# Batch 1's state softmax from token-partition scores, sums of exponentials on GpSimd, and a new order of every step

## The chip, the cores and the metric

The kernel runs on one core of one Trainium2 chip. The core has five instruction streams that run side by side and wait for each other by semaphores: TensorE (PE, with its weight loads shown apart as PEld), VectorE (DVE), ScalarE (ACT), GpSimd (POOL) and SyncE (SP, which here only issues transfers). The metric is the device time of one execution in microseconds; each time given is a median of runs.

## The reference, cut to what matters

A block with two stages. The first is a cross attention between tokens `x` (8 batches, 8 heads, 512 tokens, 64 wide) and a small state (32 rows per head): tokens read the state, and the state rows read the tokens. Both results are laid behind each other, 544 rows of 512 per batch. The second stage is a two-layer network with a leaky activation over all 4352 rows.

```python
scores = scale * x @ state.T            # per batch and head, 512 x 32
a = softmax(scores)                     # over the 32 state rows
xread = a @ state
a2 = softmax(scale * state @ x.T)       # over the 512 tokens
sread = a2 @ x
X = concat([xread, sread], rows)        # heads side by side: 544 x 512 per batch
h = X @ w_in                            # 512 -> 2048
g = max(h, 0) + alpha * min(h, 0)
out = g @ w_out                         # 2048 -> 512
```

## The kernel before, in words

All is unrolled by hand. `ORDER` is a string of some 1250 tokens; a loop at the end calls one small function per token, and manual scheduling keeps that order on every engine. So each engine runs its own instructions strictly in the order in which the tokens stand, and an instruction whose input is late holds up all that stand behind it on its engine. The last numbers of a token choose one of the eight PSUM banks or a slot of a buffer.

The work by token, with its line in the kernel before:

- Loads, issued by GpSimd (they cast to f16): `lx` one batch of `x` (L201), `wi` and `wo` a quarter of each weight (L253, L259), `lst` the states (L247). `xd` (L327) is a transfer issued by SP that writes `x` transposed into `xT`; for batches 0 and 1 TensorE transposes instead (`xt`, L340). `tt` (L541) transposes the exponentials `e2` by a transfer.
- Scores: `sc` (L362) puts the scores of one batch with states in partitions into two banks. They feed the softmax over tokens: `tm` maximum on DVE (L514), `te` exponentials on ACT (L527), then `rd` (L553) reads the tokens.
- The softmax over the 32 state rows has two forms. Batches 1 to 7 take the scores of `sc`: `sb` transposes 32x32 blocks on DVE (L466), `smax` maximum on DVE (L476), `ssh` subtracts on GpSimd (L482), `sexp` on ACT (L488). Batch 0 computes its scores a second time on TensorE with tokens in partitions: `sd` (32 small matmuls per half, L409), `hm` maximum on DVE (L420), `hs` subtracts by a matmul with a negative identity (L423), `he` on ACT (L433). Both go on with `ssum`, sum and reciprocal on DVE (L492, L493), `snorm` on GpSimd (L496) and `wb`, a block transpose on DVE (L504).
- `xread` is never formed: `m` (L590) multiplies the states with a 512-wide quarter of `w_in`, `mo` (L603) copies the result to f16 on ACT or DVE, and `F` (L620) multiplies this with the softmax weights: a first-layer tile of 128 hidden units by 512 tokens. `f` is the same in two halves (L641). `N` (L652, ACT) takes the negative part and `G` (L656, DVE) the activation. Batch 8 stands for the state rows of all batches (L629).
- The second layer of batch 0 is plain: `S` (L675), two matmuls of 512 columns each. For the other batches seven products `P` (L793, four matmuls of 256 columns) stand for eight, as in Strassen's scheme. They need sums of hidden blocks, `A` (L765, GpSimd or DVE), and sums of weight blocks, `W` (L745). `C` (L805, ACT or DVE) copies a product out, `D` (L810, DVE) adds one, and `st` (L722, SP) stores 128 rows.
- `Z` (L272) are matmuls of zeros in the first microseconds; nothing reads them.

Buffers that take turns (`xg`, `xT`, `ts`, `e2` and others) come from a pool that hands out its copies in turn.

## Time and profile before

| | |
|---|---|
| median of 3 runs | 208.99 us (208.47 to 209.76) |
| span of the profiled execution, first to last instruction | 205.4 us |
| busy: PE / DVE / ACT / POOL | 197.1 / 181.6 / 145.2 / 159.6 us |
| moved by transfers | 23.22 MB |

The profile shows one execution. The span leaves out what lies around the instructions: the median of the runs is 3.6 us above it, and the steps of the prediction are taken against the span and then carried over by these 3.6 us. An engine's busy time counts matmuls with modelled, overlapping ends, so a PE that is busy all the time can still be slowed; the distance from one matmul to the next is the better measure of its pace. In the windows below, a pair is microseconds busy and the number of instructions.

### The profile page before, as it was taken

The page shows a single profiled execution, that of the slowest core. Times are in us where ns is not written, and L with a number is a line of the kernel's source. Part 1 is how long each engine was busy: PE and PEld are TensorE (multiplying, and loading weights), DVE is VectorE, ACT ScalarE, POOL GpSimd, SP SyncE. Part 2 cuts the span into 40 slices and gives each one's busy share as a digit, 9 for nine tenths or more (in the row PEclk, how much of TensorE's full clock was granted, in tenths as well). Part 3 has the DMA queues.
Part 4 walks back from the last instruction along what each step waited for, and adds up shares of the span by engine and source line. Part 5 has one row for each costly group of instructions (what it writes and reads, how often), then busy time and mean ns, then how long its engine had stood idle before and what let it go on. Part 6 is the DMA issues. An engine that isn't in the chain of part 4 may idle for free.

```text
span 205.4 us, 5181 instructions
## 1 busy us (share of the span) xinstructions
PE 197.1 (96%) x2023; PEld 131.4 (64%) x2023; DVE 181.6 (88%) x321; ACT 145.2 (71%) x319; POOL 159.6 (78%) x136
## 2 busy tenths in 40 slices
PE   7887999999999999999999999999999999999993
PEld 2542344445757766766557776776778777788882
DVE  4799999999999989999899999989999699995841
ACT  2599997889897679899898878869666476411120
POOL 7575489999989979998998899987997988502220
PEclk9999999999999999999999999999999999999999
DMA  5999999995999342749990135022000220031124
GB/s 81 195 203 209 204 206 197 185 232 54 163 163 178 66 153 58 100 103 158 194 163 3 53 123 135 3 105 102 0 0 3 111 93 3 2 131 62 69 102 156
DMA packets 39257, 23.22 MB, mean 113 GB/s; under 512 B 22320, under 2 KB 35008, under 8 KB 39232
## 3 DMA queue, kind: packets, MB, share of 16 engines
q0 software_dynamic: 12704, 8.59, 29.3%
q1 hardware_dynamic: 26496, 14.29, 28.4%
q8 instruction: 16, 0.26, 0.6%
q14 instruction: 9, 0.07, 0.2%
q10 hardware_dynamic: 32, 0.01, 0.0%
HBM read 17.31 MB, written 8.91 MB: 128 GB/s over the span
## 4 chain that ended last, share of the span: by engine, by line
PE 85%; DVE 5%; DMA 5%; POOL 1%; ACT 1%; issue 1%; ACTq 0%; POOLq 0%
PE ps L793 44%; PE ps L620 24%; PE ps L675 7%; DMA xg<-in_x_dram 5%; PE ps L629 3%; PE ps L590 3%; DVE gt_all L656 3%; PE ps L553 1%; ACT neg_all L652 1%; PE ps L362 1%; DVE m_all L603 1%; POOL xg L218 1%; DVE ts L466 1%; DVE nb L514 1%; DVE mx L476 1%
## 5 line engine op out<-in xcount | busy, mean ns | idle before, releaser
L656 DVE SCALAR_TENSOR_TENSOR gt_all<-neg_all,oma_sb,ps 128x512 f16<-128x512 f32 x128 | 89.3, 738 | 3.0 <-ACT neg_all L652 2.7
L652 ACT ACTIVATE neg_all<-ps 128x512 f32<-128x512 f32 (+1 forms) x144 | 77.4, 598 | 20.0 <-PE ps L620 14.4
L620 PE MATMUL ps<-aT,m_all 128*128 128x512 f16 x250 | 66.4, 379 | 0.3 <-DVE m_all L603 0.2
L765 POOL TENSOR_TENSOR hc_all<-gt_all 128x512 f16<-128x512 f16 x43 | 49.2, 1160 | 11.4 <-DVE osb_all L810 8.7
L793 PEld LDWEIGHTS <-hc_all 128*128 128x128 f16 x480 | 46.3, 98 | 14.3 <-issue 1.1
L793 PE MATMUL ps<-wc,hc_all 128*128 128x256 f16 x360 | 47.7, 273 | 0.0
L793 PEld LDWEIGHTS <-gt_all 128*128 128x128 f16 x336 | 32.6, 98 | 8.3 <-issue 0.5
L805 ACT COPY osb_all<-ps 128x256 f32<-128x256 f32 x51 | 19.1, 383 | 25.7 <-PE ps L793 22.2
L620 PEld LDWEIGHTS <-m_all 128*128 128x128 f16 x250 | 24.0, 98 | 18.0 <-issue 2.2
L603 ACT CAST m_all<-ps 128x512 f16<-128x512 f32 x58 | 31.6, 621 | 4.3 <-PE ps L590 4.3
L765 POOL TENSOR_TENSOR hc_all<-gt_all,hc_all 128x512 f16<-128x512 f16 x22 | 25.4, 1164 | 6.3 <-DVE hc_all L765 6.1
L793 PE MATMUL ps<-w_out_sb,gt_all 128*128 128x256 f16 x224 | 29.7, 273 | 0.0
L765 POOL TENSOR_TENSOR hc_all<-hc_all,gt_all 128x512 f16<-128x512 f16 x21 | 24.3, 1164 | 3.9 <-DVE hc_all L765 3.6
L810 DVE TENSOR_TENSOR osb_all<-osb_all,ps 128x256 f32<-128x256 f32 x45 | 18.0, 413 | 7.6 <-PE ps L793 4.7
L496 POOL TENSOR_TENSOR an<-ts,r 128x1024 f16<-128x1024 f32 (+1 forms) x9 | 15.5, 1725 | 6.2 <-DVE r L493 4.0
L482 POOL TENSOR_TENSOR ts<-ts,mx 128x1024 f32<-128x1024 f32 x7 | 13.4, 1918 | 5.4 <-DVE mx L476 5.4
L675 PE MATMUL ps<-w_out_sb,gt_all 128*128 128x512 f16 x64 | 16.6, 380 | 0.1
L793 PE MATMUL ps<-w_out_sb,hc_all 128*128 128x256 f16 x120 | 16.5, 273 | 0.0
L793 PE MATMUL ps<-wc,gt_all 128*128 128x256 f16 x112 | 14.7, 273 | 0.0
L590 PE MATMUL ps<-w_in_sb,stT 64*32 64x512 f16 x256 | 11.8, 383 | 1.9 <-DMA w_in_sb<-in_moe_w_in_dram 0.9
L527 ACT ACTIVATE e<-ps,nb 128x512 f16<-128x512 f32 x16 | 11.1, 705 | 0.1
L675 PEld LDWEIGHTS <-gt_all 128*128 128x128 f16 x64 | 5.9, 98 | 7.2 <-issue 1.2
(78 smaller groups left out, 204.6 us busy)
## 6 DMA issues: line engine op xcount, KB each, us to landing
out_dram<-osb_all SPq DMA_DIRECT2D x33, 256.0 KB, 2.6
xg<-in_x_dram POOLq DMA_DIRECT2D x7, 512.0 KB, 9.1
w_in_sb<-in_moe_w_in_dram POOLq DMA_DIRECT2D x4, 512.0 KB, 12.0
w_out_sb<-in_moe_w_out_dram POOLq DMA_DIRECT2D x4, 512.0 KB, 13.6
xg<-in_x_dram POOLq DMA_DIRECT2D x2, 256.0 KB, 4.5
out_dram<-osb_all SPq DMA_DIRECT2D x2, 128.0 KB, 2.4
gs_all<-in_state_dram POOLq DMA_DIRECT2D x1, 192.0 KB, 6.8
st<-in_state_dram SPq DMA_DIRECT2D x1, 128.0 KB, 2.4
```

The source lines that it names most:

```text
L482: engine(e).tensor_tensor(ts, ts, over_blocks(cols(softmax_tile("mx", b), j, S // N)), ALU.subtract)
L496: engine(e).tensor_tensor(blocks(cols(softmax_tile("an", b), j, S)), blocks(cols(softmax_tile("ts", b), j, S)), over_blocks(cols(softmax_t ...
L590: nc.tensor.matmul(banks[N * k : N * (k + 1), (k0, k1)[g], :], st_head(b, 2 * k + g)[64 * g : 64 * g + 64, :], w_in_sb[64 * g : 64 * g + 6 ...
L603: copier(e)(ms[b, f][:, g, :], banks[:, live["mp", b, f][g], :])
L620: nc.tensor.matmul(h.rearrange("p (r t) -> p r t", r=2), ms[b, f][:, g, 128 * j : 128 * (j + 1)], weights(b, g), start=(g == 0), stop=(g = ...
L652: nc.scalar.activation(neg, h, RELU, bias=0.0, scale=-1.0)
L656: nc.vector.scalar_tensor_tensor(gts[b, f][:, j, :], negs.pop((b, jc)), oma_sb[:, jc : jc + 1], hs.pop((b, jc)), ALU.mult, ALU.add,)
L675: nc.tensor.matmul(outs[b, q], hidden(b, jc, q), w_out_sb[:, jc, :], start=(jc == 0), stop=(jc == n_jc - 1),)
L765: engine(e).tensor_tensor(t, x, y, ALU.add if s == 1 else ALU.subtract)
L793: nc.tensor.matmul(outs[b, i, bank], rows, cols, start=(p in (1, 2, 5) and jc == 0), stop=(jc == n_jc // 2 - 1), skip_group_check=True,)
L805: copier(e)(rows_at(b, q, k)[:, 256 * half : 256 * (half + 1)], outs[b, i, "x"])
L810: nc.vector.tensor_tensor(to, to, outs[b, i, bank], ALU.add)
```

## The change

Batch 1's softmax over the state rows takes the form that batch 0 had (`sd`, `hm`, `hs`, `he`, in two halves) in place of `sb`, `smax`, `ssh`, `sexp`; `sc.1` stays, for the softmax over tokens. The reciprocal becomes a step of its own, `srec`, and `ssum` names its engine: two of the ten sums stay on DVE (the first half of batch 0, and batch 3), eight go to GpSimd as a chain of five additions that halve the width from 32 to 1 (16, 8, 4, 2, 1), with the tile `an` as scratch. `ORDER` is replaced as a whole, so all steps of all engines stand in a new order and many change bank, slot or engine: of 120 `A`, 37 are on DVE instead of 32; of 60 `C`, 18 instead of 9; of 64 `mo`, 9 instead of 6; of 8 `W`, 2 instead of none. The zeros shrink from 21 matmuls to 15. Buffers that took turns now have fixed places in a table, `HOMES`. Functions for joint products, pairs of tiles and double stores (`CC`, `DD`, `su`, `NN`) are added, but no token of `ORDER` calls them.

```diff
-lx0.0 lx0.1 id ni.v wi.0 oma lst stc Z.7.32 stt.2 sto.a lx.1 wi.1 dd.0.0.v wi.2 Z.7.3 xt.0.0.0.6
...
+lx0.1 lx0.0 id lst stc Z.7.20 stt.0 sto.v dd.1.0.a dd.1.1.a dd.0.0.a dd.0.1.a Z.7.11 xt.0.0.1.1 xt.0.1.1.2
...
+HOMES = {
+    "xg": "01232013",
+    "xT": "01010101",
...
+    "e2": "01220120",
+    "e2T": "10001001",
+    "sn": "01000110",
+}
...
+    homes = {
+        kind: [consts.tile(shape, dtype, name=f"{kind}_{i}") for i in range(n)]
+        for kind, (n, shape, dtype) in kinds.items()
+    }
+
+    def home(kind, b):
+        return homes[kind][int(HOMES[kind][b])]
...
-    def state_sum(b, j=None):
+    def state_sum(e, b, j=None):
         r1 = cols(softmax_tile("r1", b), j, S // N)
-        nc.vector.tensor_reduce(r1, blocks(cols(softmax_tile("ts", b), j, S)), AX.X, ALU.add)
+        t = blocks(cols(softmax_tile("ts", b), j, S))
+        if e == "v":
+            nc.vector.tensor_reduce(r1, t, AX.X, ALU.add)
+            return
+        part = cols(softmax_tile("an", b), j, S).bitcast(F32)
+        w = N // 2
+        part = part.rearrange("p (c n) -> p c n", n=w)
+        nc.gpsimd.tensor_tensor(part, t[:, :, :w], t[:, :, w:], ALU.add)
+        while w > 2:
+            w //= 2
+            nc.gpsimd.tensor_tensor(
+                part[:, :, :w], part[:, :, :w], part[:, :, w : 2 * w], ALU.add
+            )
+        nc.gpsimd.tensor_tensor(
+            r1.rearrange("p (c o) -> p c o", o=1), part[:, :, :1], part[:, :, 1:2], ALU.add
+        )
+
+    def state_reciprocal(b, j=None):
+        r1 = cols(softmax_tile("r1", b), j, S // N)
         nc.vector.reciprocal(r1, r1)
```

How the new table moves instructions is shown at three places. The first is GpSimd's queue near the start. Before, from the first weight load on (`w_in_sb` and `w_out_sb` are the weights, `gs_all` first holds the states, `xg_124`, `xg_377` and `xg_443` are batches 1, 2 and 3 of `x`, `an`, `ts` and `r` belong to batch 0's softmax):

```order
L253 DMA w_in_sb<-in_moe_w_in_dram 128x4x512
L247 DMA gs_all<-in_state_dram 128x768
L201 DMA xg_124<-in_x_dram 128x8x256
L253 DMA w_in_sb<-in_moe_w_in_dram 128x4x512 x3
L496 TENSOR_TENSOR an_298<-ts_240,r_0_242 128x512 x2
L259 DMA w_out_sb<-in_moe_w_out_dram 128x4x512 x4
L201 DMA xg_377<-in_x_dram 128x8x256
L201 DMA xg_443<-in_x_dram 128x8x256
```

Now, from the first load of `w_out` on (`xg_69` is batch 2, `xg_70` batch 3, L517 to L523 are one sum of exponentials):

```order
L284 DMA w_out_sb<-in_moe_w_out_dram 128x4x512
L517 TENSOR_TENSOR an_79<-ts_73 128x256
L520 TENSOR_TENSOR an_79<-an_79 128x16x8
L520 TENSOR_TENSOR an_79<-an_79 128x16x4
L520 TENSOR_TENSOR an_79<-an_79 128x16x2
L523 TENSOR_TENSOR r_0_77<-an_79 128x16
L532 TENSOR_TENSOR an_79<-ts_73,r_0_77 128x512 x2
L284 DMA w_out_sb<-in_moe_w_out_dram 128x4x512
L226 DMA xg_69<-in_x_dram 128x8x256
L284 DMA w_out_sb<-in_moe_w_out_dram 128x4x512 x2
L226 DMA xg_70<-in_x_dram 128x8x256
```

Batch 2 of `x` was loaded behind all four quarters of `w_out`; now the last two quarters, and batch 3, stand behind it.

The second place is SP's queue, from its second transfer on. Before (`xT_628` and `xT_793` are the transposed batches 2 and 3, `e2T` the transposed exponentials of batches 0 and 1):

```order
L327 DMA_TRANSPOSE xT_628<-xg_377 128x16x128
L541 DMA_TRANSPOSE e2T_711<-e_0_307 128x8x128
L541 DMA_TRANSPOSE e2T_713<-e_1_416 128x8x128
L327 DMA_TRANSPOSE xT_793<-xg_443 128x16x128
L722 DMA out_dram<-osb_all 128x512 x2
```

Now (`xT_71` is batch 2, `xT_72` batch 3, `e2T_86` and `e2T_87` batches 2 and 0):

```order
L352 DMA_TRANSPOSE xT_71<-xg_69 128x16x128
L352 DMA_TRANSPOSE xT_72<-xg_70 128x16x128
L761 DMA out_dram<-osb_all 128x512
L575 DMA_TRANSPOSE e2T_86<-e_2_85 128x8x128
L575 DMA_TRANSPOSE e2T_87<-e_0_83 128x8x128
```

The two transposed loads come first, and only batch 2's own load releases the first of them.

The third place is TensorE, where it first reads the transposed batch 2. Before, the last steps ahead of it and its first row (`aT_550` are batch 1's softmax weights, `gt_all` the activations):

```order
L620 LDWEIGHTS m_all
L620 MATMUL ps<-aT_550,m_all 128x512
L675 LDWEIGHTS gt_all
L675 MATMUL ps<-w_out_sb,gt_all 128x512
L362 LDWEIGHTS stT
L362 MATMUL ps<-xT_628,stT 32x256
```

Now:

```order
L659 LDWEIGHTS m_all
L659 MATMUL ps<-aT_82,m_all 128x512
L714 LDWEIGHTS gt_all
L714 MATMUL ps<-w_out_sb,gt_all 128x512
L387 LDWEIGHTS stT
L387 MATMUL ps<-xT_71,stT 32x256
```

The neighbours read alike; what moved is how much stands ahead. Before, 26 first-layer steps, 20 second-layer steps and 12 `m` stood ahead of these scores; now 22, 10 and 13 do, with two more `sd` and two more `hs`.

More of the change, by code (lines that the diff above doesn't have):

```diff
@@ L769, in product @@
         bank = {1: "x", 6: "x", 7: "x", 4: "x", 2: "y", 5: "z", 3: "z"}[p]
-        if k is not None:
-            outs[b, i, bank] = single(k, 256)
+        if b in joint:
+            if k is not None:
+                both = outs[b, bank] = single(k).rearrange("p (i c) -> p i c", i=2)
+                for h in range(2):
+                    outs[b, h, bank] = both[:, h]
+            opens = k is not None
+        else:
+            if k is not None:
+                outs[b, i, bank] = single(k, 256)
+            opens = p in (1, 2, 5)
         n = n_jc // 4
@@ L796, in product @@
                 cols,
-                start=(p in (1, 2, 5) and jc == 0),
+                start=(opens and jc == 0),
                 stop=(jc == n_jc // 2 - 1),
@@ L829 @@
     }
-    for token in (globals().get("TOKENS") or ORDER).split():
+    for token in ORDER.split():
         name, *args = token.split(".")
```

299 lines of the change are left out of this document (162 added, 137 removed).

## The prediction

> **What bounds the kernel now.** I read the page for shares, the windows for where each engine is full, and the chain of waits for the pace of TensorE. The page's span, busy times and shares of the chain:
>
> ```profile
> span 205.4 us, 5181 instructions
> PE 197.1 (96%) x2023; PEld 131.4 (64%) x2023; DVE 181.6 (88%) x321; ACT 145.2 (71%) x319; POOL 159.6 (78%) x136
> PE 85%; DVE 5%; DMA 5%; POOL 1%; ACT 1%; issue 1%; ACTq 0%; POOLq 0%
> ```
>
> The windows (us; busy of PE, PEld, DVE, ACT, POOL, each with its instructions; granted clock; DMA share; GB/s):
>
> ```profile
> 10.00:20.00 10.00, 8.17 (x128) 3.70 (x128) 9.46 (x15) 9.13 (x22) 6.80 (x8) 1.00 1.30 204
> 20.00:30.00 10.00, 9.20 (x72) 3.67 (x72) 9.96 (x17) 10.00 (x22) 6.08 (x3) 1.00 1.24 207
> 30.00:40.00 10.00, 10.00 (x48) 4.54 (x47) 10.00 (x15) 7.97 (x16) 9.94 (x5) 1.00 1.28 192
> 40.00:50.00 10.00, 10.00 (x158) 4.44 (x156) 9.83 (x17) 8.72 (x20) 9.63 (x7) 1.00 0.84 155
> ```
>
> Pieces of the chain (start, length, what):
>
> ```profile
> 25.12 1.89 PE ps L675 x8
> 28.15 0.43 PE ps L620 x2
> 180.04 21.85 PE ps L793 x200
> ```
>
> A first-layer step (two L620) takes 0.43 us and the last 200 products take 21.85, 0.109 each for half the columns, so this is one and the same full pace. Up to 25.12, where the second layer starts, TensorE waits on and off for DVE (9.46 and 9.96 of 10) and ACT (9.13 and 10.00); from about 28 to 201.9 it waits for almost nothing. The span is therefore the moment at which TensorE passes a given place in its order, plus the work behind that place. What matters is when it passes, and how much work is added.
>
> **Part by part.** Everything is summed against the span of 205.4; the median of the runs, 208.99, is 3.6 more, which I carry over.
>
> *Added work on TensorE.* Batch 0's token-partition scores show what batch 1's will cost:
>
> ```profile
> L409 PE MATMUL ps<-gs_all,xT 128*32 128x64 f16 x64 | 0.8, 194 | 0.1
> L423 PE MATMUL ps<-gs_all 128*128 128x512 bf16 x2 | 0.8, 376 | 0.1
> ```
>
> 64 small matmuls cost 0.8; the two shifting ones 2 x 0.22 at the pace above (0.8 at the most, as they stand here). That is +1.2 on the bounding engine, between 0 (if they fall into a wait of the start) and +1.6. The six zero matmuls less lie in waits: 0.
>
> *The start.* DVE and ACT gate it, so what they gain there may come back:
>
> ```profile
> L466 DVE STREAM_TRANSPOSE ts<-ps 128x1024 f32<-128x1024 f32 x7 | 8.7, 1243 | 0.0
> L476 DVE TENSOR_REDUCE mx<-ts 128x32 f32<-128x1024 f32 x7 | 8.5, 1209 | 0.0
> L492 DVE TENSOR_REDUCE r<-ts 128x32 f32<-128x1024 f32 x7 | 8.5, 1215 | 0.2 <-ACT ts L488 0.2
> L317 DVE COPY stT<-ps 128x768 f16<-128x768 f16 x1 | 0.9, 905 | 0.0
> L420 DVE TENSOR_REDUCE gs_all<-ps 128x16 bf16<-128x512 f32 x2 | 1.3, 687 | 0.0
> L603 DVE CAST m_all<-ps 128x512 f16<-128x512 f32 x6 | 4.0, 682 | 0.0
> L433 ACT ACTIVATE ts<-ps 128x512 f32<-128x512 f32 x2 | 1.2, 597 | 1.2 <-PE ps L423 1.2
> ```
>
> DVE loses batch 1's transpose 1.24, maximum 1.21 and sum 1.21, half a sum of batch 0 (0.6) and the states' copy 0.91, and gains two maxima (1.37) and two more `m` casts before the first second-layer step (1.36): 5.17 less, 2.73 more, so 2.4 us freed. But ACT, full in the same stretch, takes the states' copy (about as long there, 0.9) and batch 1's two exponentials (1.2) ahead of that step, and gives up the two casts (about 1.3). ACT ends 0.8 fuller. So the return lies between 0 (ACT decides) and 2.4 (DVE decides); ACT is the fuller one by its row, and I take -0.7.
>
> *Sums on GpSimd.* Its priced neighbours:
>
> ```profile
> L496 POOL TENSOR_TENSOR an<-ts,r 128x1024 f16<-128x1024 f32 x7 | 13.4, 1918 | 2.7 <-ACT osb_all L805 1.5 <-ACT neg_all L652 0.7 <-DVE r L493 0.5
> L496 POOL TENSOR_TENSOR an<-ts,r 128x512 f16<-128x512 f32 x2 | 2.1, 1048 | 3.5 <-DVE r L493 3.5
> L765 POOL TENSOR_TENSOR hc_all<-gt_all 128x512 f16<-128x512 f16 x43 | 49.2, 1160 | 11.4 <-DVE osb_all L810 8.7 <-PE ps L574 1.5 <-PE ps L553 0.7
> L745 POOL TENSOR_TENSOR wc<-w_out_sb 128x1024 f16<-128x1024 f16 x4 | 8.5, 2130 | 0.0
> L482 POOL TENSOR_TENSOR ts<-ts,mx 128x1024 f32<-128x1024 f32 x7 | 13.4, 1918 | 5.4 <-DVE mx L476 5.4
> ```
>
> 512 more columns cost 0.87, so a column costs 1.7 ns and an instruction about 0.18 us. A whole batch's chain has 512+256+128+64+32 = 992 columns in five instructions: 1.7 + 0.9 = 2.6 us, against 1.2 on DVE; a half 0.84 + 0.9 = 1.7. Five whole and three half chains add 18. It could be as little as the columns alone (11) or, if narrow pieces cost as a 512-wide instruction does, 8 x 5 x 1.05 = 42; I take 18, by the two rows of the same kind. GpSimd gives up five `A` (5.8), two `W` (4.3) and batch 1's subtraction (1.9): net +6, 166 of some 209 us. Its sums stand a stage ahead of the first-layer steps that need them, whose cover is the products of the batch before. On the path: 0; with cover gone, it is a rival below.
>
> *Switching between small and full matmuls, buffers in fixed places, copies moved from ACT to DVE.* ACT has 29% idle and DVE keeps about its total, 0 each, give or take 0.5 together.
>
> *Batch 2's transposed load.* This decides. For TensorE, SP and GpSimd the rows are (a transfer's row, then its time to landing; the last is TensorE's first read of batch 2):
>
> ```profile
> L259 POOL DMA_DIRECT2D w_out_sb<-in_moe_w_out_dram x2: 762/766/770, 15.0 to 15.7; - x2
> DMA to landing us min/median/max: 14.5/15.4/16.3
> L201 POOL DMA_DIRECT2D xg<-in_x_dram x2: 918/920/922, 16.4 to 17.3; - x2
> DMA to landing us min/median/max: 18.3/19.3/20.3
> L327 SPq DMA_TRANSPOSE xT<-xg x1: 3023/3023/3023, 34.8 to 34.8; - x1
> DMA to landing us min/median/max: 4.6/4.6/4.6
> L327 SPq DMA_TRANSPOSE xT<-xg x1: 1800/1800/1800, 40.7 to 40.7; - x1
> DMA to landing us min/median/max: 4.3/4.3/4.3
> L201 POOL DMA_DIRECT2D xg<-in_x_dram x1: 939/939/939, 55.4 to 55.4; - x1
> DMA to landing us min/median/max: 9.1/9.1/9.1
> L327 SPq DMA_TRANSPOSE xT<-xg x1: 5753/5753/5753, 56.1 to 56.1; - x1
> DMA to landing us min/median/max: 9.6/9.6/9.6
> 41.46 0.41 PE L362 MATMUL ps<-xT,stT 64*32 64x256 f16 x16
> ```
>
> Before, the last two quarters of `w_out` land at 29.5 and 32.0, batch 2 at 34.7 and batch 3 at 37.6, one behind the other; the transposing transfer starts at 34.8, lands at 39.4, and TensorE reads it at 41.5, 2 us later. Now batch 2 is ahead of those two quarters, 2 x 2.5 us earlier: it lands at 29.7. The transposing transfer starts then, with 2.5 + 2.5 + 2.9 = 7.9 us of loads still queued. Alone it took 4.3; beside the last batch of loads 4.6; beside a whole load issued just ahead of it 9.6, and that load 9.1. I take 9.6, since more is queued here than there: landing at 39.3. The bounds are 34.0 (alone) and 41.9 (7.9 of loads first, then 4.3).
>
> The Trainium skill's page "DMA: Bandwidth & Descriptors", section "Issuing engines are not separate DMA queues", says that transfers issued by SP, ACT and GpSimd run on the same 16 DMA engines and interleave; sharing evenly would double 4.6 to an estimated 9.2 and give a time 0.4 shorter than mine. The rows agree.
>
> When does TensorE want it? Ahead of these scores stand four first-layer and ten second-layer steps less than before (14 x 0.43 = 6.0), one `m` (0.4) and the 1.2 more, less the start's 0.7: 41.5 - 6.0 + 0.4 + 1.2 - 0.7 = 36.4. Work behind them: 205.4 - 41.5 + 6.0 - 0.4 = 169.5. So TensorE stands from 36.4 to 39.3, 2.9 us, with 14 steps behind it that need nothing of batch 2. DVE's queue has batch 2's block transpose and then batch 1's remaining activations behind it, so DVE cannot work ahead meanwhile, and the time isn't won back.
>
> Sum: 205.4 + 1.2 - 0.7 + 2.9 = 208.8, that is 39.3 + 169.5; with 3.6 around it **212.4 us**.
>
> A wait of TensorE could cost more than its length. In the windows above the granted clock is 1.00 throughout, and TensorE never stands for 2.9 us there, so no row prices it. The Trainium skill's page "TensorE: Matmul & The Clock Gate", Part 1, says that an idle window of about 3.4 us halves the array's clock until it has been busy about as long. By that page a wait of 2.9 us costs nothing more, and one at the upper bound of the landing an estimated 1.7 us, half a window, on top.
>
> **Rivals.**
>
> *The transposed load is in time (no stall).* Place: the same read. It decides below a landing at 36.4, 6.7 us after the start of the transfer. For it: 4.3 and 4.6 are the commoner times here. Against: neither of these had two whole loads behind it. Then 36.4 + 169.5 = 205.9, or **209.5 us**, no change. Chance 0.25.
>
> *The start pays in full, without a stall.* DVE's 2.4 comes back whole and the added matmuls fall into waits: 205.4 - 2.4 = 203.0, **206.6 us**, faster. For it: DVE is at 9.96 to 10.00 from 20 to 40. Against: ACT at 10.00 in 20 to 30, which gets more. Chance 0.12.
>
> *GpSimd's sums are dear.* At 5.2 us a chain instead of 2.6, batches 2, 4, 5 and 6 add 10.4 between 30 and 150 us, where GpSimd idles 0.1 to 0.4 in 10 by the two windows from 30 to 50, some 3 in all; the `A` that the products wait for then come 7 us late. It decides from about 3.4 a chain, where the idle time is used up. For it: the narrow additions have no row. Against: the two rows above scale with columns. 205.9 + 7.4 = 213.3, **216.9 us**. Chance 0.08.
>
> **The numbers.** The stall of 2.9 us has 0.55; 212.4 is its time. Its bounds run from nothing to 5.5 (215.0), so its own range is 210.5 to 214.5. The range goes down to 206.5, which takes in the case without a stall and the start's full return, and up to 214.5: left out are the dear sums, the latest landings and a start better still, some 0.17. About 1%, 2.1 us, is what a measurement of this kernel can tell from no change: slower is above 211.1, faster below 206.9. Slower: 0.50 of the stall's 0.55 and the 0.08 of the sums, 0.58. Same: 0.25 and the short stalls, 0.30. Faster 0.12.
>
> **What would show it.** A stall: TensorE idle just before its first read of batch 2's `xT`, ended by the transposing transfer, 2 to 4 us long, with DVE idle in the same window, and that transfer at 9 us or more. Without it: landing within 7 us and a full PE from 30 to 40. The start: the first second-layer matmul at 26 to 27 (25.1 before, with two first-layer steps and 1.2 us more work ahead). GpSimd: five additions that sum to 2.6 per batch and a busy time near 166. I am wrong if PE is at full pace through 45 us, or if a second wait of over 1 us stands later than that.

## The result: 8% slower, and the profile after

| | before | after |
|---|---|---|
| median of 4 runs | 208.73 us (207.52 to 209.76) | 225.32 us (224.94 to 225.54) |
| ratio | | 1.080 (95% interval 1.074 to 1.086) |
| span of the profiled execution | 205.4 us | 223.8 us |
| DVE busy with `A` in 60 to 140 us | 2.64 us for 7 | 14.13 us for 15 |

The forecast was 212.4, with a range from 206.5 to 214.5. The direction was right, the time is 11 us outside the range. In this and all later runs an execution takes 1.7 to 2.0 us more than its own span; the 3.6 that the prediction carried over came from setting one short execution (span 205.4) against the median of others. Each median here is over all executions, while the ratios of the next table leave out one execution each of e3, e9, e10, e12 and e14 that took over 1.5% longer than the fastest of its kernel.

The head of the page after, with the busy times, three of its rows by slices (the span in 40 parts; `PEclk` is the clock granted to TensorE, in tenths) and the chain by engine:

```profile
PE 204.7 (91%) x2083; PEld 131.6 (59%) x2083; DVE 193.1 (86%) x332; ACT 143.8 (64%) x312; POOL 172.9 (77%) x170
PE   7879993799979989899989989999999999999993
...
DVE  3899994659999999999999999999999797958561
...
PEclk9999999589999999999999999999999999999999
...
PE 47%; DVE 35%; DMA 9%; issue 4%; ACT 3%; POOL 1%; DVEq 0%; POOLq 0%
```

Before, the chain was PE for 85% and DVE for 5%; now DVE holds 35% of it. PE has one hole (the 3 at the seventh slice), a dip of the granted clock right behind it (5 in the eighth), and then a long stretch of eights and nines with one seven, in which DVE is at nine throughout. So there are two places, and only the first was in the forecast. The windows of the profile after, with the columns of the prediction's windows, show both:

```profile
30.00:40.00 10.00, 5.37 (x25) 2.24 (x23) 6.09 (x10) 5.69 (x12) 9.21 (x5) 0.98 1.26 177
40.00:50.00 10.00, 9.56 (x46) 3.70 (x47) 6.13 (x8) 4.07 (x7) 3.07 (x2) 0.68 0.35 79
60.00:140.00 80.00, 74.09 (x791) 49.62 (x790) 79.32 (x121) 60.73 (x137) 72.73 (x64) 1.00 0.63 118
```

The same 80 us before, for the last row:

```profile
60.00:140.00 80.00, 79.85 (x883) 54.98 (x881) 76.13 (x126) 67.01 (x151) 73.62 (x62) 1.00 0.54 105
```

**The first place.** What TensorE and DVE waited for between 34 and 60 us (total, times, longest), and then the chain there (start, length, what):

```profile
PE ps L387 <- DMA xT<-xg: 5.1, 1, 5.1
DVE ts L484 <- PE ps L387: 5.0, 1, 5.0
```

```profile
29.91 10.49 DMA xT<-xg
...
40.44 0.62 PE ps L387 x12
41.06 3.53 PE ps L714 x8
```

The transposing transfer of batch 2 starts at 29.9 and lands at 40.4. TensorE has waited since 35.4. Then eight matmuls of 512 columns take 3.53 us, some 0.43 from one start to the next, in place of 0.216: the clock is at half until about 46.5. That is 1.7 us on these eight; with the six behind them, 2.7 us on top of the wait, summed from the single matmuls.

**The second place.** What TensorE waited for between 60 and 140 us:

```profile
PE ps L659 <- DVE gt_all L695: 1.8, 3, 0.9
PE ps L840 <- DVE hc_all L804: 1.7, 1, 1.7
PE ps L659 <- DVE aT L540: 1.1, 1, 1.1
```

All of it is DVE, on several lines: not one late result, but an engine that is behind. DVE's instructions at L804 (`A`) and L784 (`W`) in that stretch, by form, with the mean in ns at the end:

```profile
L804 DVE TENSOR_TENSOR hc_all<-gt_all,hc_all 128x512 f16<-128x512 f16 x5 | 5.7, 1162 | 0.0
L804 DVE TENSOR_TENSOR hc_all<-gt_all 128x512 f16<-128x512 f16 x6 | 5.0, 830 | 0.0
L804 DVE TENSOR_TENSOR hc_all<-hc_all,gt_all 128x512 f16<-128x512 f16 x4 | 3.5, 874 | 0.0
L784 DVE TENSOR_TENSOR wc<-w_out_sb 128x1024 f16<-128x1024 f16 x1 | 2.4, 2395 | 0.0
L784 DVE TENSOR_TENSOR wc<-w_out_sb,wc 128x1024 f16<-128x1024 f16 x1 | 1.1, 1116 | 0.0
```

Before, the same instruction took 0.42 us in this stretch:

```profile
L765 DVE TENSOR_TENSOR hc_all<-gt_all 128x512 f16<-128x512 f16 x3 | 1.2, 408 | 0.0
L765 DVE TENSOR_TENSOR hc_all<-gt_all,hc_all 128x512 f16<-128x512 f16 x2 | 0.8, 416 | 0.0
L765 DVE TENSOR_TENSOR hc_all<-hc_all,gt_all 128x512 f16<-128x512 f16 x2 | 0.8, 420 | 0.0
```

The timeline of DVE and GpSimd from 61.8 us on says why (start, duration, both in us):

```profile
61.84 1.49 POOL L804 TENSOR_TENSOR hc_all<-hc_all,gt_all 128x512 f16<-128x512 f16 x1
...
62.97 0.64 DVE L804 TENSOR_TENSOR hc_all<-hc_all,gt_all 128x512 f16<-128x512 f16 x1
63.29 2.09 POOL L500 TENSOR_TENSOR ts<-ts,mx 128x1024 f32<-128x1024 f32 x1
63.53 2.40 DVE L784 TENSOR_TENSOR wc<-w_out_sb 128x1024 f16<-128x1024 f16 x1
65.34 1.59 POOL L804 TENSOR_TENSOR hc_all<-gt_all 128x512 f16<-128x512 f16 x1
65.85 1.37 DVE L804 TENSOR_TENSOR hc_all<-hc_all,gt_all 128x512 f16<-128x512 f16 x1
```

The last DVE row runs from 65.85 to 67.22, and GpSimd's row above it ends at 66.93: DVE ends 0.29 later. The one at 62.97 ends at 63.61, 0.28 after GpSimd's row that began at 61.84. Of the 15 `A` between 60 and 140 us, 14 end 0.28 or 0.29 us behind a GpSimd instruction. So these DVE instructions do their work only when GpSimd's running instruction has ended, and GpSimd's next one, already started, is the longer for it (1.59 for the one that starts at 65.34, beside the `W` that ends at 65.93, in place of 1.16). In the whole trace the `A` on DVE that take 0.36 to 0.43 are those that start with no GpSimd instruction running, or with one that ends within 0.15 us. One that started 0.02 us ahead of such an end took 1.41 all the same: GpSimd's next instruction came first.

Summed over TensorE: the distance from one matmul to the next, above its pace (0.216 us for 512 columns, 0.109 for 256), comes to 2.1 us before and 20.1 after, counted from the first second-layer matmul. The 18 us between them are the span's 18.4. Of the 20.1, the first wait has 5.2, the halved clock 2.7, the stretch from 60 to 140 us 9.3 (1.5 before), all else 2.9. The single matmuls of the trace are behind these sums.

### The profile page after: what moved, and what is told of

Its sections match the earlier page's. It is cut to its first block, busy times and chain, and to the rows that moved or that the text cites. A ratio compares the mean times of both kernels' runs of the same rounds, so it can differ in the third digit from the quotient of the medians.

```text
span 223.8 us, 5345 instructions
## 1 busy us (share of the span) xinstructions
PE 204.7 (91%) x2083; PEld 131.6 (59%) x2083; DVE 193.1 (86%) x332; ACT 143.8 (64%) x312; POOL 172.9 (77%) x170
## 4 chain that ended last, share of the span: by engine, by line
PE 47%; DVE 35%; DMA 9%; issue 4%; ACT 3%; POOL 1%; DVEq 0%; POOLq 0%
PE ps L840 22%; DVE gt_all L695 14%; PE ps L659 12%; DVE hc_all L804 7%; PE ps L714 6%; DMA xT<-xg 5%; DMA xg<-in_x_dram 4%; PE ps L668 3%; DVE osb_all L857 2%; DVE nb L550 2%; PE ps L624 2%; DVE ts L484 2%; DVE aT L540 1%; ACT m_all L637 1%; DVE wc L784 1%
## 5 line engine op out<-in xcount | busy, mean ns | idle before, releaser
L691 ACT ACTIVATE neg_all<-ps 128x512 f32<-128x512 f32 (+1 forms) x144 | 78.8, 593 | 42.5 <-PE ps L659 31.7
L804 POOL TENSOR_TENSOR hc_all<-gt_all 128x512 f16<-128x512 f16 x39 | 46.5, 1202 | 3.3 <-DVE gt_all L695 2.9
L840 PEld LDWEIGHTS <-gt_all 128*128 128x128 f16 x336 | 32.5, 98 | 11.1 <-issue 2.8
L852 ACT COPY osb_all<-ps 128x256 f32<-128x256 f32 x42 | 15.8, 386 | 24.7 <-PE ps L840 17.6
L804 POOL TENSOR_TENSOR hc_all<-gt_all,hc_all 128x512 f16<-128x512 f16 x18 | 20.6, 1153 | 10.9 <-PE ps L840 5.9
L804 POOL TENSOR_TENSOR hc_all<-hc_all,gt_all 128x512 f16<-128x512 f16 x19 | 23.0, 1214 | 0.7
L714 PE MATMUL ps<-w_out_sb,gt_all 128*128 128x512 f16 x64 | 18.3, 419 | 0.0
L500 POOL TENSOR_TENSOR ts<-ts,mx 128x1024 f32<-128x1024 f32 x6 | 11.8, 1972 | 5.6 <-DVE mx L494 5.6
L517 POOL TENSOR_TENSOR an<-ts 128x512 f32<-128x512 f32 (+1 forms) x8 | 8.6, 1076 | 4.5 <-ACT ts L458 4.0
L484 DVE STREAM_TRANSPOSE ts<-ps 128x1024 f32<-128x1024 f32 x6 | 7.4, 1238 | 5.1 <-PE ps L387 5.0
L520 POOL TENSOR_TENSOR an<-an 128x128 f32<-128x128 f32 (+3 forms) x24 | 10.4, 433 | 1.9
```

The costliest lines, as they stand in the source:

```text
L484: nc.vector.transpose(softmax_tile("ts", b).rearrange("p (r s) -> p r s", r=2), sc.rearrange("p g r t -> p r (g t)"),)
L500: engine(e).tensor_tensor(ts, ts, over_blocks(cols(softmax_tile("mx", b), j, S // N)), ALU.subtract)
L691: nc.scalar.activation(neg, h, RELU, bias=0.0, scale=-1.0)
L714: nc.tensor.matmul(outs[b, q], hidden(b, jc, q), w_out_sb[:, jc, :], start=(jc == 0), stop=(jc == n_jc - 1),)
L804: engine(e).tensor_tensor(t, x, y, ALU.add if s == 1 else ALU.subtract)
L840: nc.tensor.matmul(outs[b, i, bank], rows, cols, start=(opens and jc == 0), stop=(jc == n_jc // 2 - 1), skip_group_check=True,)
```

## The experiments

Two theories stood: DVE's two-input sums wait for GpSimd (call it the waiting theory), and, as its rival, DVE simply has too much work, or GpSimd's sums of exponentials hold things up. For the first place: TensorE's pace sets the end, so the wait and the halved clock are worth their length; or DVE's later stretch sets it, and a gain ahead of it is lost again. A diff shows tokens of `ORDER`, cut to what moves; the kernel before took 207.7 to 208.2 in these comparisons.

| run | median of four, us | ratio to before (95% interval) |
|---|---|---|
| e1, scores late | 222.3 | 1.069 (1.064 to 1.073) |
| e2, zeros in the wait | 224.1 | 1.078 (1.071 to 1.086) |
| e3, one input | 218.3 | 1.048 (1.043 to 1.053) |
| e4, sums back on DVE | 232.0 | 1.114 (1.110 to 1.119) |
| e5, scores later | 223.3 | 1.074 (1.069 to 1.078) |
| e6, sums swapped | 241.1 | 1.158 (1.150 to 1.166) |
| e7, both removed | 214.5 | 1.031 (1.027 to 1.035) |
| e8, before with 14 `A` on DVE | 238.8 | 1.149 (1.144 to 1.153) |
| e9, repaired | 225.9 | 1.084 (1.081 to 1.088) |
| e10, repaired, one input | 222.9 | 1.068 (1.063 to 1.073) |
| e11, before with the scores alone | 211.8 | 1.017 (1.014 to 1.020) |
| e12, e8 with one input | 228.9 | 1.094 (1.086 to 1.103) |
| e13, `W` early | 219.3 | 1.058 (1.049 to 1.067) |
| e14, e13 with one input | 215.8 | 1.036 (1.028 to 1.044) |
| e15, load first | 224.7 | 1.080 (1.071 to 1.088) |
| e16, stores first | 220.8 | 1.059 (1.052 to 1.066) |
| e17, e16 with one input | 214.0 | 1.028 (1.022 to 1.034) |

### The first wait alone: e1, e2 and e5

e1 puts batch 2's scores behind other matmuls:

```diff
-G.0.15 sc.2.2.4.5 S.0.0.6
+G.0.15 S.0.0.6
...
-S.0.3.7 sb.2 N.1.10.0 G.1.0 F.1.5.7 smax.2 N.1.8.2
+S.0.3.7 N.1.10.0 G.1.0 F.1.5.7 N.1.8.2
...
-F.1.12.1 N.1.11.1 O.0.3.a.1 F.1.7.3 N.1.5.3 N.1.13.0
+F.1.12.1 N.1.11.1 sc.2.2.4.5 sb.2 O.0.3.a.1 F.1.7.3 smax.2 N.1.5.3 N.1.13.0 ssh.p.2
```

> Batch 2's scores (sc.2) and what hangs on them (sb.2, smax.2, ssh.2) stand some twenty steps later, so that about 4.8 us of second-layer and first-layer matmuls fill the wait for the transposing transfer. Theory 1, TensorE's pace sets the end: the 5.2 us wait goes, the granted clock stays at 1.00 in 40 to 50 us, and the 3 us of halved matmuls go with it: 225.3 - 8 = about 217. Theory 2, DVE's pace sets the end from 60 us on (10.00 of 10 busy in 60 to 100): only the 5.0 us that DVE stood idle at 35 to 41 come back: about 220. Theory 3, the time is set by later waits alone, which grow by what is gained here: 224 or more.

222.3 us, between theory 2 (220) and theory 3 (224). The clock stayed at 1.00, and TensorE waited 0.3 us for the transfer, but DVE stood before the same scores and TensorE then stood before DVE. Waits of DVE and of TensorE from 34 to 60 us in this run:

```profile
DVE ts L484 <- PE ps L387: 3.8, 1, 3.8
PE ps L714 <- DVE gt_all L695: 2.7, 1, 2.7
```

So this edit took the wait from one queue and left it in another. e2 leaves the wait and keeps TensorE busy in it:

```diff
-G.0.15 sc.2.2.4.5
+G.0.15 Z.4.88 sc.2.2.4.5
```

> 22 matmuls of zeros into a free bank stand just before batch 2's scores: 4.75 us of matmuls at 0.216 each, inside a wait of 5.2 us that stays as it is. Theory 1 (the pause halves the clock, and TensorE's pace sets the end): the granted clock stays near 1.00 in 40 to 50 us, the 14 matmuls of 0.43 take 0.216, 3 us come back: about 222.3. Theory 2 (DVE sets the end from 60 us on): the clock stays up but DVE resumes at the same 40.6 us, and the time stays 225 +- 0.7. If the clock falls all the same, the pause is not what lowers it.

224.1 us, 1.2 less than the changed kernel, and 0.2 below theory 2's range; the four executions run from 222.9 to 225.8, so the 1.2 isn't clear of their spread. The window from 40 to 50 us in this run has a granted clock of 1.00:

```profile
40.00:50.00 10.00, 9.98 (x61) 4.57 (x61) 9.17 (x12) 6.89 (x15) 5.96 (x7) 1.00 0.36 80
```

So it is the pause that lowers the clock, and full pace after it is worth little as long as DVE comes back at the same moment. e5 moves DVE's two steps further behind (against e1):

```diff
-N.1.11.1 sc.2.2.4.5 sb.2 O.0.3.a.1 F.1.7.3 smax.2
+N.1.11.1 sc.2.2.4.5 O.0.3.a.1 F.1.7.3
-N.1.5.3 N.1.13.0 ssh.p.2 G.1.8 S.0.2.0.2 S.0.2.1 sexp.2 G.1.11 F.1.15.6
+N.1.5.3 N.1.13.0 G.1.8 S.0.2.0.2 S.0.2.1 sb.2 smax.2 ssh.p.2 G.1.11 F.1.15.6 sexp.2
```

> As the run with batch 2's scores placed later, but DVE's transpose sb.2 and maximum smax.2 stand still later, behind one more activation and two more second-layer steps, so that DVE too has work while the transfer is under way (there it stood idle 3.85 us at sb.2, and TensorE then 2.7 at an activation). Theory 1, the wait of 5.2 us and the halved clock are worth their 8 us if neither engine waits: 217 to 218. Theory 2, whatever is gained here is lost again at DVE's full stretch from 60 us on: 222, as in the earlier run.

223.3 us: theory 2. DVE now waits 1.6 us at `sb.2`, but TensorE waits 1.9 at 43 us for an activation behind `sb.2` and `smax.2`, and behind that wait the clock is at half (0.83 granted over 40 to 50 us). Neither edit gets at the stretch from 60 us on.

### DVE beside GpSimd: e3 and e4

e3 keeps every place and engine, and takes one of the two inputs of the 17 early sums away, by making each a transposition of the other input (`t` in place of `v` in their tokens, values left out):

```diff
-        engine(e).tensor_tensor(t, x, y, ALU.add if s == 1 else ALU.subtract)
+        nc.vector.transpose(t.bitcast(F32), (x if s == 2 else y).bitcast(F32)) if e == "t" else engine(e).tensor_tensor(t, x, y, ALU.add if s == 1 else ALU.subtract)
```

> The 17 sums on DVE that stand before 140 us (15 A, 2 W) become transposes of the same tile read as pairs, with one SBUF input in place of two; the place in the order and the engine stay. What is left out: the values of these sums, so the products made of them are of other numbers. The 17 take 17.8 us now. Theory 1 (a DVE instruction with two SBUF inputs waits until GpSimd's running instruction ends): with one input each takes its own time, about 0.36 (W about 0.68) by 1.21 ns a column of the 1024-wide transposes, 6.8 in all; DVE gets 11 us back between 60 and 140, GpSimd's own sums no longer take 1.33, TensorE's waits of about 8 us there shrink to 1 or 2: about 218. Theory 2 (DVE is over-full by its work alone): these 17 still wait beside GpSimd, or their own share is 15 x 0.42 + 2 x 0.8 = 7.9 and 1 us comes back: 224 or more.

218.3 us: theory 1, 7.0 less. DVE's `A` from 60 to 140 us in this run, 13 of which start beside a running GpSimd instruction:

```profile
L804 DVE STREAM_TRANSPOSE hc_all<-hc_all 128x256 f32<-128x256 f32 x9 | 3.8, 430 | 0.0
L804 DVE STREAM_TRANSPOSE hc_all<-gt_all 128x256 f32<-128x256 f32 x6 | 2.5, 424 | 0.0
```

The 15 `A` take 6.3 us where they took 14.1, and none takes over 0.45. An `A` as a transposition is as long as a sum that nobody delays (0.43 and 0.42), so the work is the same and the waiting is gone. The 9 that keep `hc_all` as their input still need a sum that is made elsewhere, so it wasn't the waiting for that sum. TensorE's waits for DVE from 60 to 140 us went too. (This trace is of an execution of 223.2 us, in which TensorE also waited 4.6 us for ACT at 86 us, of which more below; the other three took 217.5 to 218.6.)

A transposition is another operation as well as one input less. The changed kernel's own trace tells the two apart: `D` is a sum of two inputs too, but one of them is in PSUM (`ps`). Of its 45, 32 start beside a running GpSimd instruction, and none takes over 0.42 us (minimum, median and maximum in ns):

```profile
L857 DVE TENSOR_TENSOR osb_all<-osb_all,ps x45: 362/408/422, 70.2 to 219.2; 128x256 f32<-128x256 f32 x45
```

So a second input in SBUF is what the sums that wait have and these lack. The type differs too (f16 there, f32 here), and no run separates that.

e4 tries the rival, GpSimd's sums of exponentials:

```diff
-ssum.p.2
+ssum.v.2
...
-ssum.p.7
+ssum.v.7
```

> The five sums of exponentials of batches 2, 4, 5, 6 and 7 go back to DVE (1.2 us each) from GpSimd (3.0 us each). Theory 1 (GpSimd's sums are what costs, by their length or by their holding DVE up): about 5 us come back: 220. Theory 2 (DVE's two-input sums wait for whatever GpSimd runs, mostly its own A): GpSimd is 15 us freer but stays busy beside DVE's A, DVE gets 6 us more and some collisions less: 224 to 227.

232.0 us, 6.7 slower than the changed kernel. Outside both expectations, on the far side from theory 1: the five sums on DVE are 6.0 us of work, and they cost that and a little more. The windows of this run from 60 to 140 us show GpSimd 8.6 us freer and DVE as full as it was:

```profile
60.00:140.00 80.00, 72.33 (x765) 47.94 (x765) 79.01 (x116) 59.15 (x133) 64.11 (x51) 0.98 0.57 106
```

This fits DVE's pace setting the end. The sums on DVE stand where GpSimd's stood, so the run gives their price at these places alone; there the sums on GpSimd were the cheaper ones.

### Both, and the kernel before made to collide: e7, e8 and e12

e7 joins the edits of e5 and e3.

> Both suspected losses taken away at once: the scores of batch 2 later, and the 17 sums on DVE with one input (values of these sums left out, as before). Theory 1 (the two account for the loss, and hide each other when only one is removed): 218.3 with one input alone, less the 5.2 us wait and about 2.5 of halved clock: 210 to 211, that is, the kernel before plus the added matmuls and what is left of waits near the end. Theory 2 (a third loss stands behind them): 214 or more.

214.5 us. Together they are worth 10.8, more than 2.0 and 7.0 apart: each hid part of the other. But it lies in theory 2's range, 3.5 above what theory 1 gave. The longest of TensorE's waits from 30 to 140 us in this run are not those of the changed kernel: 1.9 us for an activation of DVE's and 0.8 for ACT.

e8 asks the same of the kernel before: every fourth `A` of GpSimd's between 55 and 140 us goes to DVE.

```diff
-A.1.0.4.0.p.0
+A.1.0.4.0.v.0
...
-A.5.0.4.0.p.1
+A.5.0.4.0.v.1
```

> The kernel before, in which 14 of the 54 A that GpSimd makes between 55 and 140 us, every fourth, go to DVE at the same place; nothing else. Theory 1 (a two-input sum on DVE waits for GpSimd's running instruction): they take about 0.95 each as in the changed kernel, most of those beside a running GpSimd instruction ending about 0.3 after it; DVE gets 13 us more in a stretch where it has 4 to spare of 80: 214 to 218. Theory 2 (a sum costs DVE 0.42 wherever it stands, as this kernel's own did): 6 us more on DVE, GpSimd 16 us freer: 207 to 211.

238.8 us, 31 slower, far over both. Theory 2 is out, but theory 1's sum is too small as well. The timeline of DVE and GpSimd at the longest wait:

```profile
58.46 2.26 POOL L765 TENSOR_TENSOR hc_all<-gt_all 128x512 f16<-128x512 f16 x2
58.58 5.39 DVE L765 TENSOR_TENSOR hc_all<-hc_all,gt_all 128x512 f16<-128x512 f16 x1
60.68 1.14 POOL L765 TENSOR_TENSOR hc_all<-hc_all,gt_all 128x512 f16<-128x512 f16 x1
61.79 1.90 POOL L482 TENSOR_TENSOR ts<-ts,mx 128x1024 f32<-128x1024 f32 x1
```

The sum on DVE took 5.39 us: it waited through four GpSimd instructions and ended 0.28 after the last, at 63.97. It is not one of the 14. It is `A.1.0.2.0`, which DVE made in the kernel before too, in 0.42 us at 57.6, when GpSimd stood still because its next sum, `A.1.0.4.0`, needs this one. e8 gives `A.1.0.4.0` to DVE, so GpSimd no longer stands still and runs on. Of the 14 moved sums seven waited, 7 us in all; with the 5 us of `A.1.0.2.0` that is 12. That doesn't make 31. GpSimd and TensorE also wait for sums that DVE makes, by the waits of this run:

```profile
PE ps L793 <- DVE hc_all L765: 19.9, 8, 4.2
POOL hc_all L765 <- DVE hc_all L765: 15.0, 7, 5.1
```

Before, GpSimd's waits for DVE's sums were 9.7 us, and TensorE had none of 0.3 us or more. Behind the waits the clock fell too (0.89 granted from 60 to 140 us).

e12 tells the two apart, with one input for the 14 (against e8):

```diff
-A.1.0.4.0.v.0
+A.1.0.4.0.t.0
...
-A.5.0.4.0.v.1
+A.5.0.4.0.t.1
```

> The kernel before with the same 14 A at DVE's place as in the run that took 238.8 us, but with one SBUF input (values left out). In that run eight of them waited for GpSimd, 12 us in all, one 5 us through four GpSimd instructions; GpSimd in turn waited 15 us for A that DVE made later in its queue. Theory 1 (the waiting of two-input sums is the loss, and the long waits and the lowered clock follow from it): 210 to 216. Theory 2 (the hand-over between the two engines is: GpSimd's next A needs the one that DVE makes late): 228 or more. Between the two, both.

228.9 us: theory 2's side, but 10 of the 31 went. `A.1.0.2.0` keeps its two inputs here, and its wait is the same. Its row in the timeline, and then TensorE's waits in this run for sums that DVE makes:

```profile
57.69 5.39 DVE L765 TENSOR_TENSOR hc_all<-hc_all,gt_all 128x512 f16<-128x512 f16 x1
```

```profile
PE ps L793 <- DVE hc_all L765: 15.1, 6, 4.2
```

So the waiting of two-input sums is at least a third of e8's loss. How the rest divides among the wait that stayed (TensorE stood 4.2 us for it), sums that stand late in DVE's queue and the lowered clock (0.94 from 60 to 140 us) is not shown. That sums stand late is: TensorE waited 2.9 us at 115 us for a moved one that took 0.44. e8 by itself would have borne out the waiting theory with a wrong number.

### Repairs, and what the rest is: e6, e9, e10 and e13 to e17

e6 gives the 17 early sums to GpSimd and five sums of exponentials to DVE:

```diff
-A.1.1.2.0.v.1
+A.1.1.2.0.p.1
...
-ssum.p.2
+ssum.v.2
```

> The 15 A and 2 W on DVE before 140 us go to GpSimd (15 x 1.16 + 2 x 2.13 = 21.7 us), and the sums of exponentials of batches 2, 4, 5, 6, 7 come back to DVE (5 x 1.2 = 6 us for 15 on GpSimd). Theory 1 (DVE's waits for GpSimd are the loss): DVE gets 17.8 - 6 = 12 us back, GpSimd gets 4 us fuller in 60 to 140 (73.7 of 80 now), TensorE's waits for DVE go: 218 to 219. Theory 2 (both engines together have too much to do in this stretch): GpSimd becomes the late one, TensorE waits for its sums instead, and the time stays within 2 of 225.

241.1 us. Theory 2's side, and far beyond it: GpSimd is now the late one, and TensorE waits 19.5 us in all for sums that it makes.

e9 starts from late scores (`sb.2` behind `F.1.15.6`, `smax.2` behind `G.1.5`) and takes 6.8 us off DVE:

```diff
-W.2.1.p G.1.3
+W.2.1.p W.3.1.p W.0.0.p G.1.3
...
-mo.0.2.v.1.7 mo.0.2.v.0
+mo.0.2.a.1.7 mo.0.2.a.0
...
-mo.0.3.v.0.8
+mo.0.3.a.0.8
```

> The changed kernel with its computation whole and three edits to its order: batch 2's scores late, with sb.2 and smax.2 on DVE behind the activations for which TensorE waited 2.0 us in the run before; the two W of DVE (3.5 us with their waits) on GpSimd in its idle stretch at 41 to 46 us; five m copies from DVE (5 x 0.67) to ACT. Theory 1 (DVE's pace from 60 us on sets the end): 223.3 - 3.5 - 3.3 - 2 = 214 to 215. Theory 2 (what is taken from DVE comes back as waits for ACT or GpSimd): 219 or more.

225.9 us: no gain. The fault is in the edit: three of the five `m` copies stand ahead of the first second-layer step, where ACT was full already, and that step began at 29.6 us, 4.1 later than in the changed kernel.

> The same, and the 15 A on DVE before 140 us with one input in place of two (their values left out). Theory 1 (beside the late scores, only the waits of two-input sums for GpSimd's instruction cost time): TensorE's waits between 30 and 170 us fall to those of the kernel before, and the time to that of before plus at most 3: 209 to 211. Theory 2 (a third loss): 213 or more.

222.9 us, with the same late start (28.8); it says nothing about a third loss. It does bear out one step of the prediction, that ACT decides the start. e13 leaves the copies alone, with the scores as in e5:

```diff
-W.2.1.p G.1.3
+W.2.1.p W.3.1.p W.0.0.p G.1.3
```

> The changed kernel, computation whole, with batch 2's scores as in the run that took 223.3 us, and DVE's two W on GpSimd in its idle stretch near 40 to 46 us; the m copies stay (moving them to ACT held up the start by 4 us). Theory 1 (DVE's pace from 60 us on sets the end, and its waits for GpSimd make that pace): DVE loses 3.5 us of work and waits: 219 to 220. Theory 2 (GpSimd pays for it): 222 or more.

219.3 us: theory 1, and a whole kernel that is 6.0 faster than the changed one. GpSimd had the time to spare between 40 and 46 us, and DVE lost two instructions that took 3.5 us.

> The same with the 15 A on DVE before 140 us on one input (values left out). Against the run with both losses removed (214.5, TensorE waiting 2.0 us at 42, 0.7 at 50, and 1.8 for ACT at 82), DVE has another 1.4 us less. Theory 1 (what is left is the order near 40 to 85 us, not a loss of its own): 212 to 214.5. Theory 2 (a further loss on DVE or GpSimd): 216 or more.

215.8 us, between the two. TensorE waits less for DVE than in e13 and more for ACT at 82 us. What ACT waited for there in e14:

```profile
ACT osb_all L852 <- DMA out_dram<-osb_all: 4.1, 1, 4.1
```

ACT's copy needs a buffer whose store has not been issued: in SP's queue four stores stand behind `xd.5`, which itself waits until its load lands at 78.9. The same wait, 6.3 us of ACT's, stands in the traced execution of e3; the changed kernel's TensorE has none for ACT there. e16 and e17 put two of the stores ahead of that transfer, and five second-layer steps ahead of the step that waited at 42:

```diff
-rd.0.6 lx.5 xd.5 P.1.0.6.1
+rd.0.6 lx.5 P.1.0.6.1
...
-st.1.0 C.2.0.1.a.1
+st.1.0 xd.5 C.2.0.1.a.1
...
-G.1.11 F.1.15.6
+G.1.11 S.0.2.2 S.0.2.3 S.0.2.4 S.0.2.5 S.0.2.6 F.1.15.6
```

> The run of 219.3 us (computation whole, scores late, W early on GpSimd) with two more edits to the order: batch 5's transposing transfer on SP behind two stores instead of ahead of four, and five second-layer steps of batch 0 ahead of the first-layer step that waits 2.0 us for DVE at 42. Theory 1 (the stores held on SP by a transfer whose load is late are what ACT and then TensorE wait for at 82 to 86, 1.9 us there): both waits go, 215 to 216. Theory 2 (DVE's waits for GpSimd take it back): 218 or more.

> The same with the 15 A on one input (values left out), against 215.8 before these two edits, where TensorE waited 2.0 at 42, 1.4 at 50, and 3.5 at 82 to 86. Theory 1 (these are the rest of the loss): 210 to 211.5, the kernel before plus 2 to 3. Theory 2 (something else remains): 213 or more.

220.8 and 214.0 us. In e17 ACT's wait for a store is gone, and the median is 1.8 us under e14's, with intervals that overlap. The wait at 42 is not gone; it stands at 47 now, 2.0 us long, for the same activation, since DVE has fallen behind there. In e16, with the two-input sums, there is no gain over e13 (219.3, intervals overlap). No version here beats the kernel before.

### The transfer, and the scores alone: e15 and e11

e15 puts batch 2's load and its transposing transfer ahead of the second quarter of `w_out`:

```diff
-wo.1 mo.3.0.a.1
+lx.2 xd.2 wo.1 mo.3.0.a.1
...
-m.0.1.1.5 lx.2 xd.2 wo.2
+m.0.1.1.5 wo.2
```

> The changed kernel with batch 2's load and its transposing transfer one load earlier in GpSimd's queue, ahead of the second quarter of w_out. The load lands at 27.2 instead of 29.8, and SP starts the transfer there. Theory 1 (beside queued loads the transfer takes about 10.5 us whenever it starts): it lands at 37.8, the wait falls from 5.2 to 2.6 us, the clock stays up, TensorE gains 5 us, of which DVE's later stretch takes back some: 221 to 223. Theory 2 (it ends only with the loads that are queued at its start): it lands at 39.5 or later and the time stays within 1.5 of 225.

224.7 us, theory 2. The transfer in the changed kernel and the load of batch 3, the last in GpSimd's queue (each a row, then its time to landing):

```profile
L352 SPq DMA_TRANSPOSE xT<-xg x1: 5322/5322/5322, 29.9 to 29.9; - x1
DMA to landing us min/median/max: 10.5/10.5/10.5
L226 POOL DMA_DIRECT2D xg<-in_x_dram x1: 933/933/933, 17.3 to 17.3; - x1
DMA to landing us min/median/max: 22.1/22.1/22.1
```

The same two in e15:

```profile
L352 SPq DMA_TRANSPOSE xT<-xg x1: 6718/6718/6718, 27.1 to 27.1; - x1
DMA to landing us min/median/max: 13.9/13.9/13.9
L226 POOL DMA_DIRECT2D xg<-in_x_dram x1: 931/931/931, 18.3 to 18.3; - x1
DMA to landing us min/median/max: 22.2/22.2/22.2
```

The load lands at 39.4 and the transfer 1.0 later, at 40.4; in e15 at 40.5 and 41.0. Starting 2.8 us sooner, it took 3.4 longer. In both it ends just behind the last load that was queued when it began.

e11 puts one part of the change into the kernel before: batch 1's scores with tokens in partitions.

```diff
-te.1.0 te.1.1 m.0.2.0.3
+te.1.0 te.1.1 sd.1.0.5 sd.1.1.6 m.0.2.0.3 hm.1.0 hm.1.1
...
-sexp.1 ssum.1 snorm.p.1
+ssum.1.0 snorm.p.1.0 ssum.1.1 snorm.p.1.1
```

> The kernel before, with one part of the change alone: batch 1's softmax over the state rows from scores with tokens in partitions, in two halves, with its sums on DVE; the order of all else is kept. By the first term of the forecast the 68 matmuls more cost 0.8 to 1.6 us: 208.9 to 209.7 against 208.1. The rival, DVE's relief (2.4 us less on it near 30 us) pays for them: 207.5 to 208.3. If a wait comes of it: above 210.

211.8 us, above 210: a wait came of it. The added matmuls stood in banks that ACT still read, and TensorE waited for that, by its waits from 14 to 28 us:

```profile
PE ps L409 <- ACT e L527: 3.0, 1, 3.0
```

Taken off, the part costs about 0.6 us, an estimate; the run doesn't give the price cleanly.

## Why the prediction was right in direction and wrong in size

**The stall: right place, mis-sized.** It was forecast at the first read of batch 2's transposed `x`, with DVE idle beside it, and that is where it is. TensorE came at 35.4 (36.4 forecast) and the data at 40.4 (39.3): 5.1 to 5.2 us instead of 2.9. Of the 2.2 us more, half is TensorE's earlier arrival and half the later data: the term of the transfer's length, 9.6 by the row of a transfer beside one load, measured 10.5, from a start at 29.9 and not 29.7. A length was the wrong thing to carry over: e15 shows that the transfer ends just behind the last queued load, whenever it starts, and that load landed at 39.4 and not at 37.6. The row of before had the same sign: that transfer landed at 65.7, 1.2 us behind the load issued just ahead of it (64.5). The Trainium skill's page "DMA: Bandwidth & Descriptors", section "Issuing engines are not separate DMA queues", says that such transfers interleave; from it the prediction worked out an estimated 9.2 for an even share. The trace shows 10.5 here and 13.9 in e15, so an even share isn't what these two got.

**The halved clock: named, not counted.** The prediction left it out because a wait of 2.9 us stood below the 3.4 of the Trainium skill's page "TensorE: Matmul & The Clock Gate", Part 1. The wait was 5.1 and the clock fell, for 2.7 us of lost pace (1.7 estimated), as the Trainium skill's page has it for waits that long. e2 shows the pause as its cause. Alone neither was worth its length: full pace behind the wait gave 1.2 us (e2, within its spread), no wait and full pace 3.0 (e1). New waits took part of the rest (2.7 us in e1, 1.9 and a halved clock in e5), and, as the sum of e7 suggests, DVE's later stretch took more.

**"DVE keeps about its total, 0, give or take 0.5": the step that failed.** The changed table has five more `A` and two `W` on DVE; I showed no row for them and let them cancel against what DVE gave up. The `A` rows of before (0.42) would not have warned me: in that trace 30 of the 32 `A` on DVE start where GpSimd runs nothing, some of them because GpSimd waits for that very sum. In the new order 15 `A` (7 before) and two `W` stand between 60 and 140 us, where GpSimd is busy 9 of 10, and take 17.6 us instead of some 8 (15 x 0.42, and two of twice the width). e3 takes the second input away and with it 7.0 us of the kernel's time. What is left in e3 is still 4.8% slower than the kernel before, so the direction didn't hang on this term; the size did. What I needed was not the mean of a group but its spread, and what ran on the other engine meanwhile. The Trainium skill's page "SBUF — State Buffer", section "SBUF: two separate sides", says that DVE and GpSimd share one pair of ports as an exclusive lock, that a DVE instruction with two SBUF inputs needs it against a GpSimd instruction that reads SBUF, and that the loser blocks for the whole instruction. The traces agree (the end 0.28 us behind GpSimd's, in 0.5 to 2.1 us in the changed kernel and up to 5.4 in e8, instead of 0.42), and by that rule the forecast had a rival missing: about +10 on DVE in a stretch where it had 4 us of 80 to spare.

**The start: nearly right.** The second-layer matmuls of batch 0 in the changed kernel, with the first and the last start in us behind their three durations:

```profile
L714 PE MATMUL ps<-w_out_sb,gt_all x64: 379/379/634, 25.5 to 59.4; 128*128 128x512 f16 x64
```

25.5, where 26 to 27 was forecast. With the matmuls ahead of it and behind it counted at their pace, TensorE's own work and the start together moved the span by an estimated 0.2 us, where +0.5 was forecast. That ACT is the one that is full there was right too: e9 gave it three more copies and lost 4.1 us.

**Sums on GpSimd: right that they are covered.** Its eight chains in the changed kernel:

```profile
L517 POOL TENSOR_TENSOR an<-ts 128x512 f32<-128x512 f32 (+1 forms) x8 | 8.6, 1076 | 4.5 <-ACT ts L458 4.0 <-ACT ts L506 0.5
L520 POOL TENSOR_TENSOR an<-an 128x128 f32<-128x128 f32 (+3 forms) x24 | 10.4, 433 | 1.9
L523 POOL TENSOR_TENSOR r<-an 128x32 f32<-128x32 f32 (+1 forms) x8 | 1.8, 228 | 0.6
```

That is 20.8 us and not 18, and GpSimd is busy 172.9 and not 166. A whole chain takes 3.0, below the 3.4 from which the rival of dear sums was to decide, so that rival is out by its own condition; e4, where taking five of them back costs 6.7 us, points the same way.

**The rivals.** No stall and a full start are out by the wait row. The sign that would make the forecast wrong, a second wait of over 1 us behind 45 us, did appear, twice (1.7 and 1.1).

**What stays open.** Of the 16.6 us, the two places account for 10.8 by e7 (214.5) and 11.3 by e17 (214.0, with SP's stores moved too). Against the kernel before in their own comparisons these two are still 6.5 and 6.3 us longer. In e17 some 3 of them stand in TensorE's waits between 41 and 53 us, which two other orders of the same steps moved and did not remove, and some 2 in a slower pace behind 140 us, where DVE's sums kept two inputs and five of them still wait (0.73 to 1.42 us each). That a better order there would bring the kernel back to 208 is argued, not shown.

## What to carry to other kernels

Price a moved instruction by the instructions that will run beside it on the other engines, and read the spread of its group (minimum, median, maximum) before its mean: 0.42 us became 0.94 with no change of shape. A DVE sum of two SBUF operands belongs where GpSimd is idle, or on GpSimd, or has to be paid at the length of GpSimd's instruction. Before moving such a sum off GpSimd, ask whether GpSimd's waiting for it, or for its input, is what kept another DVE sum undisturbed (`A.1.0.2.0` in e8). When one wait is taken away and the time barely moves, look for the engine that was waiting at the same place (here DVE), and take both away in one run before judging either.

## What the runs showed of the hardware that I had not expected

- A two-input DVE instruction may lose to several GpSimd instructions in a row: 5.39 us through four of them in e8 and again in e12, where GpSimd's next followed at once each time. In the changed kernel most waited for one alone, and one for two (1.41 us). What decides between the two was not tried.
- A shorter pause can lower the clock, and need not. The waits of 4.6 to 5.3 us in the changed kernel, e3 and e4 halved TensorE's pace, for 1.7 to 2.7 us of loss. A wait of 1.9 us at 42 to 43 us halved it in e5 and e13 (some eight matmuls, 1.7 to 2.0 us) and not in e7 or e14; 2.4 us in e16 did, 2.7 us in e1 did not.
- A transposing transfer that SP issues beside loads that GpSimd has queued ends 0.5 to 1.2 us after the last of these loads: 0.5 in e15 (13.9 us after its start, against 4.3 to 5.3 for the run's other five of the same size), 1.0 in the changed kernel, 1.2 beside a single load in the kernel before.
